# Seeding the first output of FFN layer 1 in PSUM from weight pair 3 on

## The chip, the cores and the metric

The kernel runs on one core of a Trainium2 chip. Its time is the device time of one execution in microseconds (us). Three runs of the kernel before took 1123.45, 1124.03 and 1124.14 us; the median, 1124.03 us, is the number that a change is held against. The engines are called as in the profile: PE (TensorE, matrix products; PEld is its weight load), DVE (VectorE), ACT (ScalarE), POOL (GpSimd), SP (SyncE, which issues the transfers).

## What is computed

One transformer block on 2048 tokens of width 576, in float32: a layer norm, then, side by side, a local attention (32 heads of 18, each token looks at 8 earlier tokens in steps of 2) and a feed-forward net with Mish, both added to the input.

```python
x = A_x
xn = _layernorm(x, axis=-1)
return x + _A_ref(xn, A_wqkv, A_wo) + _B_ref(xn, B_w1, B_b1, B_w2)

def _B_ref(x, w1, b1, w2):          # D = 576, F = 4608
    h = jnp.einsum("bsd,df->bsf", x, w1) + b1
    sp = jnp.log1p(jnp.exp(-jnp.abs(h))) + jnp.where(h > 0, h, jnp.zeros_like(h))
    act = h * jnp.tanh(sp)
    return jnp.einsum("bsf,fd->bsd", act, w2)
```

## The kernel before

**Halves, pairs, parts.** The tokens are worked through in two halves of 1024 (`hf` 0 and 1). In each half come first the products for q, k and v, then FFN layers 1 and 2 in 18 steps, one for each pair of weight blocks (`q` from 0 to 17, 256 of the 4608 columns each), and at the very end the output product of both halves. Every float32 factor is split into a high and a low part, so that one logical product of two row blocks is six matmuls (high·high, high·low, low·high, for two blocks): `prod`. The 64 rows that are left of 576 are two matmuls more: `rest`.

**Seven products instead of eight.** Within a pair, layer 1 makes four outputs (two blocks of 512 tokens, `b`, by two weight blocks, `j`), by Strassen's scheme in Winograd's form. `m1_part` issues its six parts. In part 0, a *shared product* goes into the PSUM bank `h1`, ACT copies it to SBUF (`take`, the tile `c11`), and a *second product* with its rest goes into another bank, `h2`. The first output is the sum of the two: `mish` is handed the bank and the copy, DVE adds the bank into the copy (L702), ACT applies Mish with the bias to the copy (L703), ACT casts its high part (L708) and POOL subtracts for the low part (L709). Part 1 puts the first of another pair of products, made with the weight sum `t1`, into the bank `h3`. Parts 2 to 5 go on adding into `h1` and `h3`; on the way two more copies of `h1` are taken (`c21`, `c22`) and added the same way. The last output of a pair needs no add: there `mish` is called without a copy (`fresh`), and Mish reads the bank itself. In pairs 1 to 8 of the second half (`seven`), the outputs stay unsplit in fixed SBUF tiles (`raw_act`), because layer 2 has a Strassen scheme of its own there (`u_high` on ACT and `u_low` on DVE or POOL make its factors, `p_item` its products).

**What sets the order.** Each engine works through its own queue in the order of the program. The program is a list, `plan`, of items for PE: the parts of layer 1 mixed with chunks of layer 2 (`m2_pair`, `m2_cols`, `p_item`). For q from 1 on, most pairs have parts 0 and 1 side by side and then chunks between the others. Everything else is hung on these items with `before(i, fn)`: casts of the next pair's weights, transfers, and the steps of the attention, which POOL, DVE and ACT work on beside the FFN. The steps of the attention are spread by a sum over the items' lengths (`PART` for the parts of layer 1), in `cuts`. An attention step's exponential goes into the list `soon` and is issued at the head of the next item. What `mish` does after its matmuls goes into `pend` and is issued at the next item, ahead of that item's own matmuls:

```python
    for i, (fns, bg, _) in enumerate(plan):
        first, soon[:] = soon[:], []
        held, pend[:] = pend[:], []
        for fn in first + bg + (fns + held if i == at["m", 0, 1, 0] else held + fns):
            fn()
```

So at part 0 of a pair, ACT's queue holds: an exponential if one is due, the casts that hang on this item, Mish and cast of the last output of the pair before, and then the copy of the shared product.

**PSUM.** `bank` draws from four banks ("h"): `h1` for the whole pair, `h2` and `h3` for a part of it; the fourth is the `h1` of the pair before or after. The layer 2 products have four banks of their own ("out"), which DVE empties with adds (L759, L853, L871).

Of the kernel before, what the change touches and what calls it, by code (L numbers as in the profile page):

```python
# [39 lines left out]
def block_kernel(ctx: ExitStack, tc: tile.TileContext, x, wq, wo, w1, b1, w2, mask, out):  # L40
    nc = tc.nc
# [605 lines left out]
    cur = {}  # L647
    late = []

    def bank(hf, q, n):  # L650
        cur[n] = ps.tile([P, TB], F32, tag="h", bufs=4, name=f"h{n}_{hf}_{q}")
        return cur[n]

    def prod(ph, wt, off, X, hi, lo, first, last):
        seq = [(off + k, wl, xs + k) for k in range(2) for wl, xs in ((0, hi), (0, lo), (1, hi))]
        for i, (wk, wl, xs) in enumerate(seq):
            nc.tensor.matmul(ph, wt[:, wl, wk * P:(wk + 1) * P], X[:, xs, :],  # L657
                             start=first and i == 0, stop=last and i == len(seq) - 1,
                             skip_group_check=True)

    def rest(ph, wt, off, X, xs):
        for wl in range(2):
            nc.tensor.matmul(ph, wt[:, wl, off * P:(off + 1) * P], X[:, xs, :], start=False, stop=wl == 1,  # L663
                             skip_group_check=True)

    seven = lambda hf, q: hf == 1 and q <= 2 * OC
    rawact, rslot, held_, owner, where = {}, {}, {}, {}, {}

    def raw_act(q, b, j):
        if not rslot:  # L670
            for n in range(4):
                rslot["raw", n] = sb.tile([P, 5 * P], F32, tag="raw", bufs=4, name=f"ra{n}")
            for n in range(5):
                rslot["mn", n] = sb.tile([P, D], F32, tag="mn", bufs=5, name=f"rm{n}")
            for n in range(2):
                rslot["tt", n] = sb.tile([P, 4 * P], F32, tag="tt", bufs=2, name=f"rt{n}")
        tag, n = {(0, 0): (("raw", 0), ("raw", 1), ("raw", 2)), (1, 0): (("mn", 2), ("mn", 3), ("mn", 0), ("r3", 0)),
                  (0, 1): (("raw", 3), ("mn", 4), ("mn", 1)), (1, 1): (("tt", 0), ("tt", 1))}[b, j][q % {(1, 0): 4, (1, 1): 2}.get((b, j), 3)]
        if (tag, n) not in rslot:
            rslot[tag, n] = sb.tile([P, 2 * 432], F32, tag="r3", bufs=1, name="ra_r")  # L680
        rawact[q, b, j] = rslot[tag, n][:, 0:TB]
        owner[tag, n] = q, b, j
        where[q, b, j] = tag, n
        return rawact[q, b, j]

    def take(hf, q, name):
        if seven(hf, q):
            t = cur[name] = raw_act(q, *dict(c11=(0, 0), c21=(1, 0), c22=(1, 1))[name])
        else:
            t = cur[name] = sb.tile([P, TB], F32, tag="mn", bufs=5, name=f"{name}_{hf}_{q}")  # L690
        nc.scalar.copy(t, cur[1])  # L691

    def mish(hf, q, b, j, ph, t=None):
        f = 2 * (Q1[q] if hf else q) + j
        n = f"{hf}_{b}_{f}"
        fresh = t is None
        if fresh:
            t = raw_act(q, b, j) if seven(hf, q) else sb.tile([P, TB], F32, tag="mn", bufs=5, name=f"mn_{n}")

        def run():  # L700
            if not fresh:
                nc.vector.tensor_tensor(out=t, in0=ph, in1=t, op=ALU.add)  # L702
            nc.scalar.activation(t, ph if fresh else t, AF.Mish, bias=b1c[:, f:f + 1])  # L703
            if seven(hf, q):
                held_[q, f"A{b + 1}{j + 1}"] = f"A{b + 1}{j + 1}"
                return
            a = acts[hf, q, b, j] = sb.tile([P, 2, TB], F32R, tag=f"a{b}", bufs=(3, 2)[b], name=f"act_{n}")
            nc.scalar.copy(a[:, 0, :], t)  # L708
            nc.gpsimd.tensor_tensor(out=a[:, 1, :], in0=t, in1=a[:, 0, :].bitcast(F32), op=ALU.subtract)  # L709
        if q or b != j:  # L710
            pend.append(run)
        else:
            late.append(run)

    def m1_part(hf, q, part):
        X0, X1 = XTs[hf, 0], XTs[hf, 1]
        if part == 5 and late:
            for fn in late[::-1]:
                fn()
            late.clear()  # L720
        wa, wc, t0, t1 = (done.get((k, hf, q)) for k in ("wa", "wc", "t0", "t1"))
        if part == 0:
            prod(bank(hf, q, 1), wa, 0, X0, 0, 5, True, True)
            take(hf, q, "c11")
            prod(bank(hf, q, 2), wa, 2, X0, 2, 7, True, False)
            rest(cur[2], wa, 4, X0, 4)
            mish(hf, q, 0, 0, cur[2], cur["c11"])
        elif part == 1:
            prod(bank(hf, q, 3), t1, 0, X1, 0, 5, True, True)
        elif part == 2:  # L730
            prod(cur[1], t0, 2, Ss[hf, 1], 0, 2, False, True)
            take(hf, q, "c21")
        elif part == 3:
            prod(cur[1], t0, 0, Ss[hf, 0], 0, 2, False, False)
            rest(cur[1], wc, 2, X1, 4)
            take(hf, q, "c22")
        elif part == 4:
            prod(cur[3], t1, 2, X1, 2, 7, False, False)
            rest(cur[3], wa, 4, X1, 4)
            mish(hf, q, 1, 0, cur[3], cur["c21"])  # L740
        else:
            prod(cur[1], wc, 0, Ss[hf, 2], 0, 2, False, False)
            rest(cur[1], wc, 2, X1, 9)
            mish(hf, q, 0, 1, cur[1])
        if part == 3:
            mish(hf, q, 1, 1, cur[3], cur["c22"])
# [388 lines left out]
    plan = []  # L1135
    at = {}
    US = {"q": 2.75, "z": 2.5, "p": 3.15, "t": 0.6, "o": 2.6}
    PART = (3.2, 1.4, 1.4, 1.8, 1.8, 1.8)

    def add(tag, *fns, alias=None):  # L1140
        at[tag] = at[alias] = len(plan)
        plan.append((list(fns), [], PART[tag[3]] if tag[0] == "m" else US[tag[0]]))

    def before(i, fn):
        plan[max(i, 0)][1].append(fn)
# [1 line left out]
    def qi(hf, g, b, jj, alias=None):  # L1147
        add(("q", hf, g, b, jj), lambda: qkv_item(hf, g, b, jj), alias=alias)

    def zi(jj, part):  # L1150
        add(("z", jj, part), lambda: z_part(1, jj, part))

    def mi(hf, q, part, alias=None):
        add(("m", hf, q, part), lambda: m1_part(hf, q, part), alias=alias)
# [337 lines left out]
    for n in range(2 * steps):  # L1492
# [4 lines left out]
        hf = n // steps  # L1497
# [86 lines left out]
```

## Time and profile before

| | before |
|---|---|
| median of three runs | 1124.03 us (1123.45 to 1124.14) |
| span of the profiled execution, first to last instruction | 1121.6 us |
| median less span | 2.4 us |
| DVE, ACT, POOL busy | 74%, 44%, 70% of the span |
| adds of a copy and a bank (L702) | 108 in all: 3 for each of 36 pairs |
| weight pairs with q of 3 or more | 15 in each half, 30 in all |

The page gives no time of its own for the profiled execution; its span is set against the median, and the 2.4 us between them are taken as what lies around the span. In the lists below a row of the timeline gives start, length, engine, line, operation, output and inputs, shape and count; in brackets stands how long the engine had been idle before, and what it waited for. A row of the waits gives engine, line, what was waited for, the total in us, how many times, and the longest.

### The profile page before, as it was taken

What the parts mean: (1) busy time and instruction counts of PE and PEld (TensorE: products, weight loads), DVE (VectorE), ACT (ScalarE), POOL (GpSimd) and SP (SyncE); (2) the same over time, 40 slices, a digit from 0 to 9 for tenths busy, and PEclk for the clock granted to TensorE, in tenths of its full rate; (3) what the DMA queues carried; (4) which work ended last, traced back from release to release, by engine and by line L of the source; (5) the groups of instructions that cost most, each with busy time, mean ns of one, the idle gap of its engine ahead of it and who ended that gap; (6) DMA issues with size and microseconds to landing.
All of it is one profiled execution on the core that took longest, in us unless ns stands there. A gap on an engine that the chain in (4) does not pass through costs nothing.

```text
span 1121.6 us, 18415 instructions
## 1 busy us (share of the span) xinstructions
PE 1109.5 (99%) x6630; PEld 1023.0 (91%) x6630; DVE 829.0 (74%) x1351; ACT 492.1 (44%) x892; POOL 787.7 (70%) x639
## 2 busy tenths in 40 slices
PE   8999999999999999999999999999999999999998
PEld 7999899999999999899999889999999999999998
DVE  6368788888888888877655456687866677776876
ACT  5544645544554545455233355343433343443332
POOL 2488767767689687676788476665789878668632
PEclk9999999999999999999999999999999999999999
DMA  6899885868767849666596797655655477676463
GB/s 200 283 312 318 290 283 205 289 228 284 261 240 258 282 163 345 222 240 214 191 342 238 231 373 249 241 200 174 227 198 189 168 263 269 215 253 248 157 222 104
DMA packets 147487, 271.08 MB, mean 242 GB/s; under 512 B 30114, under 2 KB 86724, under 8 KB 147396
## 3 DMA queue, kind: packets, MB, share of 16 engines
q1 hardware_dynamic: 147396, 269.91, 69.2%
q8 instruction: 52, 0.85, 0.3%
q14 instruction: 39, 0.32, 0.1%
HBM read 160.39 MB, written 109.48 MB: 241 GB/s over the span
## 4 chain that ended last, share of the span: by engine, by line
PE 89%; DVE 4%; POOL 3%; DMA 2%; issue 1%; ACT 1%; DVEq 0%; POOLq 0%; SPq 0%
PE h L657 28%; PE po L755 19%; PE pq L349 11%; PE po L868 10%; PE po L847 7%; PE h L663 5%; PE o L1056 4%; PE z L447 2%; DMA acc<-in_x 1%; POOL accP L856 1%; DVE u L801 1%; POOL pr L534 0%; DVE accP L871 0%; POOL act L709 0%; DMA z_B<-kept_wq 0%
## 5 line engine op out<-in xcount | busy, mean ns | idle before, releaser
L755 PEld LDWEIGHTS po<-w,act 128*128 128x128 f32 x1728 | 236.4, 188 | 7.5 <-DVE acc L759 1.7
L755 PE MATMUL po<-w,act 128*128 128x288 f32 x1728 | 240.8, 295 | 1.4 <-DVE acc L759 1.2
L534 POOL TENSOR_TENSOR pr<-q,kv 128x576 f32<-128x576 f32 x128 | 195.7, 1553 | 18.7 <-DMA q<-q_d 16.9
L572 POOL TENSOR_TENSOR pv<-L,kv 128x576 f32<-128x576 f32 x128 | 174.3, 1461 | 38.7 <-DVE L L565 20.9
L709 POOL TENSOR_TENSOR act<-c,act 128x512 fp32r<-128x512 f32 x81 | 107.1, 1322 | 128.4 <-ACT act L708 125.5
L759 DVE TENSOR_TENSOR acc<-po,acc 128x288 f32<-128x288 f32 x288 | 120.4, 450 | 31.6 <-PE po L755 30.2
L349 PE MATMUL pq<-wq,xt 128*128 128x432 f32 x672 | 136.2, 361 | 1.8 <-ACT xt L83 1.8
L868 PEld LDWEIGHTS po<-w,act 128*128 128x128 f32 x960 | 131.1, 188 | 3.7 <-DVE accP L871 0.4
L868 PE MATMUL po<-w,act 128*128 128x288 f32 x960 | 133.8, 295 | 0.2
L349 PEld LDWEIGHTS pq<-wq,xt 128*128 128x128 f32 x672 | 125.0, 188 | 8.7 <-ACT xt L83 2.7
L703 ACT ACTIVATE c<-c,b1c 128x512 f32<-128x512 f32 x81 | 58.7, 724 | 132.9 <-DVE c L702 132.6
L657 PE MATMUL h<-xt,t 128*128 128x512 f32 x432 | 110.6, 391 | 0.9 <-DVE c L702 0.8
L657 PE MATMUL h<-S,t 128*128 128x512 f32 x432 | 110.4, 391 | 0.0
L691 ACT COPY c<-h 128x512 f32<-128x512 f32 x81 | 47.4, 586 | 136.5 <-PE h L663 78.3
L578 DVE TENSOR_REDUCE og<-pv 128x144 f32<-128x1152 f32 x64 | 85.9, 1343 | 25.4 <-POOL pv L572 25.4
L657 PE MATMUL h<-xt,wa 128*128 128x512 f32 x432 | 104.0, 390 | 0.0
L657 PEld LDWEIGHTS h<-xt,wa 128*128 128x128 f32 x432 | 80.9, 188 | 16.9
L871 DVE TENSOR_TENSOR accP<-po,accP 128x288 f32<-128x288 f32 x160 | 69.6, 454 | 36.1 <-PE po L868 34.5
L847 PEld LDWEIGHTS po<-pw,u 128*128 128x128 f32 x672 | 92.4, 188 | 2.9 <-DVE u L801 0.5
L847 PE MATMUL po<-pw,u 128*128 128x288 f32 x672 | 94.2, 296 | 0.3 <-DVE u L801 0.3
L539 DVE TENSOR_REDUCE L<-pr 128x64 f32<-128x1152 f32 x64 | 85.8, 1341 | 11.2 <-POOL pr L534 11.1
L657 PEld LDWEIGHTS h<-xt,t 128*128 128x128 f32 x432 | 79.0, 188 | 16.1 <-DVE c L702 1.1
(231 smaller groups left out, 1840.5 us busy)
## 6 DMA issues: line engine op xcount, KB each, us to landing
kv<-kv_d SPq DMA_DIRECT2D x64, 396.0 KB, 5.2
kept_t<-t SPq DMA_DIRECT2D x36, 512.0 KB, 5.3
t<-kept_t SPq DMA_DIRECT2D x36, 512.0 KB, 5.4
rw<-in_w SPq DMA_DIRECT2D x36, 320.0 KB, 4.6
kept_wa<-wa SPq DMA_DIRECT2D x18, 640.0 KB, 3.5
kept_w<-w SPq DMA_DIRECT2D x20, 576.0 KB, 4.8
wa<-kept_wa SPq DMA_DIRECT2D x18, 640.0 KB, 6.1
w<-kept_w SPq DMA_DIRECT2D x20, 576.0 KB, 4.5
```

The source lines that it names most:

```text
L349: nc.tensor.matmul(pq[:, 0:432], XT[:, xi, tok], wt[wi][:, hl, 0:432], start=i == 0, stop=i == len(seq) - 1)
L534: nc.gpsimd.tensor_tensor(out=pr[:, x:x + hh], in0=q[:, j0 + x:j0 + x + hh, None, :].to_broadcast([P, hh, W, CU]), in1=win(kt, 0, CU, j0 + ...
L539: nc.vector.tensor_reduce(L[:, k, j0:j0 + hj].rearrange("p j w h -> p (j w h)"), pr.rearrange("p j w (h d) -> p (j w h) d", h=2), axis=AX, ...
L572: nc.gpsimd.tensor_tensor(out=pr[:, x:x + hj].rearrange("p j d w -> p j w d"), in0=L[:, k, x:x + hj, :, h:h + 1].to_broadcast([P, hj, W, DH]),
L578: nc.vector.tensor_reduce(og[:, :, c0:c0 + DH], pr, axis=AX, op=ALU.add)
L657: nc.tensor.matmul(ph, wt[:, wl, wk * P:(wk + 1) * P], X[:, xs, :], start=first and i == 0, stop=last and i == len(seq) - 1, skip_group_ch ...
L709: nc.gpsimd.tensor_tensor(out=a[:, 1, :], in0=t, in1=a[:, 0, :].bitcast(F32), op=ALU.subtract)
L755: nc.tensor.matmul(po, acts[hf, q, b, j][:, al, tok], done["w2", hf, 2 * q + j][:, wl, c * HC:(c + 1) * HC], start=i == 0, stop=i == 5)
L759: nc.vector.tensor_tensor(out=t, in0=po, in1=t, op=ALU.add)
L847: nc.tensor.matmul(po, units[e, k, qq][:, al, tok], w[:, qq, wl, :], start=i == 0, stop=i == 5)
L868: nc.tensor.matmul(po, acts[hf, q, b, j][:, al, tok], done["w2", hf, 2 * q + j][:, wl, c * HC:(c + 1) * HC], start=i == 0, stop=i == 5)
L871: nc.vector.tensor_tensor(out=t, in0=po, in1=t, op=ALU.add)
```

## The change

From pair 3 on (`seeded`), in both halves, part 0 ends after the shared product: ACT copies it from `h1` into the PSUM bank `h2`, not into SBUF. The second product and its rest move behind the product of part 1 and add into `h2` without a first matmul that starts the sum afresh. Mish is then called without a copy and reads `h2`. DVE's add of `c11` is gone in these 30 pairs. In `add`, the lengths of parts 0 and 1 change places for them, so that the sum that spreads the attention steps follows the moved matmuls.

```diff
     seven = lambda hf, q: hf == 1 and q <= 2 * OC
+    seeded = lambda q: q >= 3
...
         if part == 0:
             prod(bank(hf, q, 1), wa, 0, X0, 0, 5, True, True)
+            if seeded(q):
+                nc.scalar.copy(bank(hf, q, 2), cur[1])
+                return
             take(hf, q, "c11")
             prod(bank(hf, q, 2), wa, 2, X0, 2, 7, True, False)
             rest(cur[2], wa, 4, X0, 4)
             mish(hf, q, 0, 0, cur[2], cur["c11"])
         elif part == 1:
             prod(bank(hf, q, 3), t1, 0, X1, 0, 5, True, True)
+            if seeded(q):
+                prod(cur[2], wa, 2, X0, 2, 7, False, False)
+                rest(cur[2], wa, 4, X0, 4)
+                mish(hf, q, 0, 0, cur[2])
...
-        plan.append((list(fns), [], PART[tag[3]] if tag[0] == "m" else US[tag[0]]))
+        part = tag[3] ^ 1 if tag[0] == "m" and tag[3] < 2 and seeded(tag[2]) else tag[-1]
+        plan.append((list(fns), [], PART[part] if tag[0] == "m" else US[tag[0]]))
```

What this does to the queues is shown at three places. The names are the program's with a running number behind them: `h1_0_4` is the bank `h1` of half 0, pair 4. First PE at the start of pair 4 of half 0, before:

```order
L657 MATMUL h1_0_4_2225<-xt_0_0_231,wa_0_4_1960 128x512 x6
L657 MATMUL h2_0_4_2234<-xt_0_0_231,wa_0_4_1960 128x512 x6
L663 MATMUL h2_0_4_2234<-xt_0_0_231,wa_0_4_1960 128x512 x2
L657 MATMUL h3_0_4_2253<-xt_0_1_515,t1_0_4_2131 128x512 x6
L755 MATMUL po_0_3_1_0_0_2268<-w2_0_6_1927,act_0_1_6_2163 128x288 x3
```

and PE at the same place now:

```order
L657 MATMUL h1_0_4_2224<-xt_0_0_231,wa_0_4_1951 128x512 x6
L657 MATMUL h3_0_4_2238<-xt_0_1_515,t1_0_4_2130 128x512 x6
L657 MATMUL h2_0_4_2231<-xt_0_0_231,wa_0_4_1951 128x512 x6
L663 MATMUL h2_0_4_2231<-xt_0_0_231,wa_0_4_1951 128x512 x2
L763 MATMUL po_0_3_1_0_0_2266<-w2_0_6_1927,act_0_1_6_2162 128x288 x3
```

The same 20 matmuls stand before the first layer 2 matmul; the six into `h3` have moved ahead of the eight into `h2`. The same place on ACT, before (the first rows belong to an attention step that falls here: a table load, the exponential, and the table load back to Mish):

```order
L559 ACTIVATE L_0_1_1605<-L_0_1_1605 128x256
L256 CAST w2_0_8_2213<-rw2_8_2070 128x576
L703 ACT_TABLE_LOAD
L703 ACTIVATE mn_0_0_7_2211<-h1_0_3_1939,b1c_126 128x512
L708 CAST act_0_0_7_2222<-mn_0_0_7_2211 128x512
L691 COPY c11_0_4_2232<-h1_0_4_2225 128x512
L256 CAST wa_0_5_2246<-rw1_10_2135 128x640
L703 ACTIVATE c11_0_4_2232<-c11_0_4_2232,b1c_126 128x512
```

and ACT now:

```order
L559 ACTIVATE L_0_1_1605<-L_0_1_1605 128x256
L256 CAST w2_0_8_2212<-rw2_8_2069 128x576
L704 ACT_TABLE_LOAD
L704 ACTIVATE mn_0_0_7_2210<-h1_0_3_1939,b1c_126 128x512
L709 CAST act_0_0_7_2221<-mn_0_0_7_2210 128x512
L726 COPY h2_0_4_2231<-h1_0_4_2224 128x512
L256 CAST wa_0_5_2236<-rw1_10_2134 128x640
L256 CAST w2_0_9_2254<-rw2_9_2132 128x576
L704 ACTIVATE mn_0_0_8_2253<-h2_0_4_2231,b1c_126 128x512
```

The copy keeps its place behind the exponential and the last output of pair 3; only what it writes is another, and Mish on the first output comes one cast later. The third place is PE at pair 9 of half 1, where a layer 2 item, the products of `u_3_6_0` and `u_3_6_1`, lies between parts 0 and 1. Before:

```order
L657 MATMUL h1_1_9_9183<-xt_1_0_6031,wa_1_10_8828 128x512 x6
L657 MATMUL h2_1_9_9192<-xt_1_0_6031,wa_1_10_8828 128x512 x6
L663 MATMUL h2_1_9_9192<-xt_1_0_6031,wa_1_10_8828 128x512 x2
L847 MATMUL po_3_6_0_0_9224<-pw_3_6_9078,u_3_6_0_9090 128x288 x3
L847 MATMUL po_3_6_0_0_9224<-pw_3_6_9078,u_3_6_1_9092 128x288 x3
```

and now:

```order
L657 MATMUL h1_1_9_9162<-xt_1_0_6016,wa_1_10_8808 128x512 x6
L855 MATMUL po_3_6_0_0_9189<-pw_3_6_9057,u_3_6_0_9069 128x288 x3
L855 MATMUL po_3_6_0_0_9189<-pw_3_6_9057,u_3_6_1_9071 128x288 x3
L855 MATMUL po_3_6_0_1_9197<-pw_3_6_9057,u_3_6_0_9069 128x288 x3
L855 MATMUL po_3_6_0_1_9197<-pw_3_6_9057,u_3_6_1_9071 128x288 x3
```

The layer 2 item now comes right behind the six matmuls of the shared product, eight matmuls earlier than before.

On DVE, 30 rows are gone. The exponentials keep their places on ACT. A few attention steps move by an item or two: on POOL in pairs 8, 15 and 16 of half 0, on DVE a reduction (L578) in pair 15 of half 0, which stood ahead of four adds of layer 2 (L759) and now stands behind them. SP issues a few of the attention transfers some places later.

## The prediction

> **What bounds the kernel now.** I read the busy line of the page first, then the waits of PE, then PE's and ACT's timelines around the shared product.
>
> ```profile
> PE 1109.5 (99%) x6630; PEld 1023.0 (91%) x6630; DVE 829.0 (74%) x1351; ACT 492.1 (44%) x892; POOL 787.7 (70%) x639
> ```
>
> PE is busy in 1109.5 of 1121.6 us and its matmuls stay the same 6630. So the time moves only where PE waits: a new wait adds its whole length, a wait that goes takes its length away, and work that goes from DVE is worth nothing by itself. Two of the waits of before lie where the change reaches (waits: engine, line, what was waited for, total, count, longest):
>
> ```profile
> PE po L755 <- DVE acc L759: 1.2, 1, 1.2
> ...
> PE po L847 <- DVE u L801: 0.3, 1, 0.3
> ```
>
> An ordinary pair, pair 5 of half 0, on PE's and ACT's timelines:
>
> ```profile
> 212.74 2.88 PE L657 MATMUL h<-xt,wa 128*128 128x512 f32 x12
> 215.46 0.62 PE L663 MATMUL h<-xt,wa 128*128 128x512 f32 x2
> ```
> ```profile
> 214.30 0.59 ACT L691 COPY c<-h 128x512 f32<-128x512 f32 x1
> ```
>
> Twelve matmuls issue in 215.46 - 212.74 = 2.72 us, 0.227 each. The shared product is the first six (1.36 us). The copy ends at 214.89, which is 2.15 us after the pair's first matmul. Today PE doesn't need it. With the change the second product adds on top of the copy, so its first matmul waits for it; ahead of it stand the shared product and the six of part 1, 2 x 1.36 = 2.72 us. **The rule for each of the 30 pairs:** the copy must end by the pair's start + 2.72 us, and what is missing PE waits. Pair 5 keeps 0.57 us. The latest of the pairs without a table load ahead of the copy is pair 10:
>
> ```profile
> 333.36 2.88 PE L657 MATMUL h<-xt,wa 128*128 128x512 f32 x12
> ```
> ```profile
> 335.26 0.58 ACT L691 COPY c<-h 128x512 f32<-128x512 f32 x1
> ```
>
> Its copy ends 335.84 - 333.36 = 2.48 us after the start: 0.24 to spare.
>
> **Removed: 30 adds on DVE.**
>
> ```profile
> L702 DVE TENSOR_TENSOR c<-h,c 128x512 f32<-128x512 f32 x81 | 55.4, 686 | 33.1 <-ACT c L691 17.9 <-PE h L663 14.2
> ```
>
> 30 x 0.686 = 20.6 us less on DVE. DVE isn't the bound, and it comes back into step with PE at the next add of a layer 2 bank; so I cost this at nothing by itself, and count only where PE waits for DVE (below).
>
> **Added: a copy from PSUM to PSUM.** No row shows one. The nearest is the same copy to SBUF, 0.586 us on average, and I take that. The ends that I keep are 0.42 (the 128x256 activation in the list below) and 1.2, twice the row, as if PSUM at both ends cost double. At 0.42 each of the four late copies below would come 0.17 earlier, 0.6 us together. At 1.2 each of the four would come 0.6 later (2.4 us), and some 26 others would miss their place by 0.1 (0.61 more against some 0.5 us to spare; 2.4 us): 4.8 us.
>
> **Moved: the second product behind part 1.** Three kinds of place. (i) In most pairs nothing waits, as in pair 5. (ii) In four pairs ACT comes late. The clearest is pair 4 of half 0; PE, then ACT, then two rows of DVE:
>
> ```profile
> 188.66 2.88 PE L657 MATMUL h<-xt,wa 128*128 128x512 f32 x12
> ```
> ```profile
> 190.86 0.42 ACT L559 ACTIVATE L<-L 128x256 f32<-128x256 f32 x1 [1.99 <-DVE L L555]
> 191.19 0.66 ACT L256 CAST w<-rw 128x576 fp32r<-128x576 f32 x1
> 191.86 1.28 ACT L703 ACT_TABLE_LOAD   x1
> 193.16 0.69 ACT L703 ACTIVATE mn<-h,b1c 128x512 f32<-128x512 f32 x1
> 193.88 0.62 ACT L708 CAST act<-mn 128x512 fp32r<-128x512 f32 x1
> 194.41 0.58 ACT L691 COPY c<-h 128x512 f32<-128x512 f32 x1
> ```
> ```profile
> 172.42 0.46 DVE L759 TENSOR_TENSOR acc<-po,acc 128x288 f32<-128x288 f32 x1 [0.34 <-PE po L755]
> ...
> 190.40 0.43 DVE L555 TENSOR_TENSOR L<-L,m 128x256 f32<-128x256 f32 x1
> ```
>
> An exponential (L559) stands ahead of the copy, waits 1.99 us for DVE, and brings a table load behind it. The copy ends at 194.99; wanted is 188.66 + 2.72 = 191.38. **Wait: 3.61 us.** Would the exponential come earlier, with DVE's add of pair 3 gone? DVE waited for PE at 172.42, behind that add, so what the add leaves is lost again there; the add of pair 4 stands behind L555. I say no. What is queued behind ACT's copy (casts, Mish of the first output) is late by nothing, since the copy keeps its place. The three others, PE first, then ACT:
>
> ```profile
> 309.21 2.88 PE L657 MATMUL h<-xt,wa 128*128 128x512 f32 x12
> ...
> 453.91 2.88 PE L657 MATMUL h<-xt,wa 128*128 128x512 f32 x12
> ...
> 872.01 2.89 PE L657 MATMUL h<-xt,wa 128*128 128x512 f32 x12
> ```
> ```profile
> 311.45 0.58 ACT L691 COPY c<-h 128x512 f32<-128x512 f32 x1
> ...
> 456.60 0.58 ACT L691 COPY c<-h 128x512 f32<-128x512 f32 x1
> ...
> 876.29 0.57 ACT L691 COPY c<-h 128x512 f32<-128x512 f32 x1
> ```
>
> Pair 9 of half 0: 312.03 against 311.93, 0.10. Pair 15 of half 0: 457.18 against 456.63, 0.55. Pair 11 of half 1: 876.86 against 874.73, 2.13. There too DVE fell back into step with PE just before:
>
> ```profile
> 870.35 0.46 DVE L871 TENSOR_TENSOR accP<-po,accP 128x288 f32<-128x288 f32 x1 [0.28 <-PE po L868]
> ```
>
> (iii) In pair 9 of half 1 a layer 2 item lies between parts 0 and 1 and now starts eight matmuls sooner, while DVE still makes its factor:
>
> ```profile
> 820.21 2.89 PE L657 MATMUL h<-xt,wa 128*128 128x512 f32 x12
> ```
> ```profile
> 820.92 1.41 DVE L801 TENSOR_TENSOR u<-ra,u 128x512 fp32r<-128x512 f32 x1
> ```
>
> The item starts at 820.21 + 1.36 = 821.57; its third matmul, two steps of 0.13 later, needs the low part that DVE ends at 822.33: 0.49 us. The new waits: 3.61 + 0.10 + 0.55 + 2.13 + 0.49 = **6.88 us**.
>
> **Waits that go.** First pair 15 to 16 of half 0, PE and then DVE:
>
> ```profile
> 461.62 1.53 PE L657 MATMUL h<-S,t 128*128 128x512 f32 x6
> 464.40 3.46 PE L755 MATMUL po<-w,act 128*128 128x288 f32 x24 [1.25 <-DVE acc L759]
> ```
> ```profile
> 458.56 1.35 DVE L578 TENSOR_REDUCE og<-pv 128x144 f32<-128x1152 f32 x1 [2.40 <-POOL pv L572]
> ```
>
> PE could have gone on at 461.62 + 1.36 = 462.98 and did so at 464.40: 1.42 us. DVE's add was late because the reduction ahead of it waited 2.40 us for POOL. Now the reduction stands behind these adds, and the add of the copy is gone too. What is late next is the reduction's result, which the end of the attention needs far later. Second, in half 1, where DVE's add waited for PE and `u` stood behind it:
>
> ```profile
> 748.30 0.82 PE L847 MATMUL po<-pw,u 128*128 128x288 f32 x5
> 749.41 1.88 PE L847 MATMUL po<-pw,u 128*128 128x288 f32 x12 [0.29 <-DVE u L801]
> ```
> ```profile
> 747.21 0.69 DVE L702 TENSOR_TENSOR ra<-h,ra 128x512 f32<-128x512 f32 x1 [2.21 <-PE h L663]
> ```
>
> Five matmuls of 0.13 end the issue at 748.96, so 0.45 us goes. Together **1.87 us**; the sum of waits is 6.88 - 1.87 = +5.0 us.
>
> **PE's clock behind the longest wait.** Rows of the windows (us, busy of PE, PEld, DVE, ACT, POOL, granted clock, transfers):
>
> ```profile
> 1.34:4.92 3.58, 3.58 (x17) 3.58 (x18) 1.13 (x5) 0.66 (x1) 0.00 (x0) 1.00 0.82 241
> 4.92:1121.08 1116.16, 1105.91 (x6615) 1019.43 (x6613) 827.40 (x1347) 490.84 (x891) 786.97 (x633) 1.00 0.70 242
> 1121.08:1121.60 0.52, 0.00 (x0) 0.00 (x0) 0.00 (x0) 0.00 (x0) 0.00 (x0) 0.50 0.00 0
> 462.33:465.75 3.42, 2.17 (x14) 1.71 (x13) 3.42 (x7) 2.19 (x5) 3.25 (x5) 1.00 0.98 324
> ...
> 1117.66:1121.08 3.42, 0.70 (x6) 0.46 (x4) 0.59 (x2) 0.00 (x0) 0.00 (x0) 1.00 0.35 123
> ```
> ```profile
> 1117.93 0.43 PE L1056 MATMUL o<-wo_r,ob 128*128 128x288 f32 x2
> ```
>
> The clock is 1.00 until 1121.08 and then 0.50, 2.72 us after the last matmul ended (1118.36). So PE idle for 2.7 us can halve the clock; 3.42 us with PE busy in 2.17 did not. The new wait of 3.61 us is longer than the one, the 2.13 us of pair 11 lie between. At the start PE ran 17 small matmuls at 3.58/17 = 0.21 us for 3.58 us; if a return to full speed again takes as long, and up to 3.61 - 2.72 = 0.9 us of it still lies in the wait, the drop costs half of 2.7 to 3.6, 1.3 to 1.8. I take **1.6 us**, once, behind pair 4. [...]
>
> **The sum:** +5.0 + 1.6 = +6.6 us on the profiled execution: 1121.6 + 6.6 = 1128.2, and with the 2.4 us that the median has above the span 1130.6 us.
>
> **The rivals.**
> 1. The clock stays. [...] Then 1130.6 - 1.6 = 1129.0 us.
> 2. The copy into PSUM is dear: at 1.2 us the 4.8 from above come on top, 1135.4 us.
> 3. Not slower: DVE, 20.6 us lighter, runs ahead and hands the exponentials over sooner. The price is ACT's 1.99 us idle before L559 and what is like it in pair 11. It decides from the point where L555 ends at 188.9 and not 190.83; then pair 4 waits 3.61 - 1.9 = 1.7 us, the clock stays, and if pair 11 is covered likewise (2.13 - 1.9 = 0.2), the waits are 1.7 + 0.10 + 0.55 + 0.2 + 0.49 = 3.0 against 1.87: +1.2, 1125.2 us. Against it stand the waits of DVE for PE at 172.42 and 870.35.
> 4. All the copies are in time, since the waits shift the queues against each other; only the gains stay: 1124.03 - 1.87 = 1122.2, or with more waits for DVE gone below 1121.8.
>
> **How the numbers follow.** Forecast (clock falls once, or in pair 11 too, 1132) 0.50; rival 1 0.30; rival 2 0.03; rival 3 0.11; rival 4 0.06, of which I put 0.04 below 1121.8. A change of 0.2%, 2.25 us, is about what a measurement can tell from none: slower 0.83 (forecast, rivals 1 and 2), same 0.13 (rival 3 and 0.02 of rival 4), faster 0.04. The range of 8 in 10 holds the forecast and rival 1. At the low end stands rival 1 with copies of 0.42 and a gain of 1 us uncounted, 1127.2, and a part of rival 3: 1126.3. At the high end stand a second drop and copies somewhat dearer than 0.586: 1132.8.
>
> **What the profile after would show.** Right: among PE's waits a new one of PE `h` for ACT `h` with its longest near 3.6 us and a next one near 2.1; one of about 0.5 for `u`; none for `acc` near 466; 78 adds of a copy on DVE instead of 108; a granted clock below 1.00 for about 3 us near 195. Wrong: PSUM copies far from 0.59 us, or no PE wait at pairs 4 and 11, which would mean that the exponentials moved; or waits of PE in ordinary pairs such as 5, which would mean that the 2.72 us of cover don't hold.

## The result, and the profile after

| | before | after |
|---|---|---|
| median, five runs each | 1124.14 us (1123.45 to 1124.54) | 1130.94 us (1129.45 to 1133.48) |
| ratio | | 1.0066, 95% interval 1.0055 to 1.0077 |
| span of the profiled execution | 1121.6 us | 1127.7 us |

The kernel is 6.8 us slower. The page's line of the busy times, of after:

```profile
PE 1110.1 (98%) x6630; PEld 1023.0 (91%) x6630; DVE 818.9 (73%) x1321; ACT 490.4 (43%) x892; POOL 789.4 (70%) x639
```

DVE has lost 30 instructions and 10.1 us of busy time. That is half of the 20.6 us that the 30 adds made up; the other half came back in other rows, as in the adds of layer 2 into `acc` (122.7 us instead of 120.4) and L257 on `wq` (14.4 instead of 11.9). PE's 6630 matmuls are busy for 1110.1 us, 1109.5 before. The profiled execution took 1129.45 us, 1.8 us more than its span; so of the 2.4 us that were taken as lying around the span of before, some 0.6 are the distance of that execution from its median (the fastest of the three took 1123.45). The forecast doesn't change by this, since it is a difference on top of the median. The difference is in PE's waits (engine, line, what was waited for, total, count, longest):

```profile
PE h L657 <- ACT h L726: 5.6, 3, 3.4
PE o L1064 <- DVE y L1068: 1.8, 3, 0.7
...
PE h L657 <- DVE rt L703: 1.2, 1, 1.2
...
PE po L855 <- DVE u L809: 0.4, 1, 0.4
```

and the row for `y` of before:

```profile
PE o L1056 <- DVE y L1060: 1.3, 2, 0.7
```

The two waits of before that the prediction quotes (`acc` 1.2, `u` 0.3 near 749) are not there; in their place stand three waits for ACT's copy into `h`, one for `u` in another pair, and two that nobody had foreseen (`rt` and the third `y`). Pair 4 of half 0 on PE and then ACT, of after:

```profile
188.18 1.52 PE L657 MATMUL h<-xt,wa 128*128 128x512 f32 x6
189.54 1.52 PE L657 MATMUL h<-xt,t 128*128 128x512 f32 x6
194.47 1.66 PE L657 MATMUL h<-xt,wa 128*128 128x512 f32 x6 [3.40 <-ACT h L726]
```
```profile
190.30 0.42 ACT L559 ACTIVATE L<-L 128x256 f32<-128x256 f32 x1 [1.98 <-DVE L L555]
190.62 0.66 ACT L256 CAST w<-rw 128x576 fp32r<-128x576 f32 x1
191.29 1.28 ACT L704 ACT_TABLE_LOAD   x1
192.59 0.69 ACT L704 ACTIVATE mn<-h,b1c 128x512 f32<-128x512 f32 x1
193.31 0.62 ACT L709 CAST act<-mn 128x512 fp32r<-128x512 f32 x1
193.83 0.58 ACT L726 COPY h<-h 128x512 f32<-128x512 f32 x1
```

The shared product and the six of part 1 issue until 189.54 + 1.36 = 190.90; the second product starts at 194.47. The chain on ACT is the one of before, with the same wait for DVE at its head (1.98 us, 1.99 before). The other long wait is in pair 11 of half 1, PE and then ACT:

```profile
875.37 1.53 PE L657 MATMUL h<-xt,wa 128*128 128x512 f32 x6
876.75 1.52 PE L657 MATMUL h<-xt,t 128*128 128x512 f32 x6
880.00 1.66 PE L657 MATMUL h<-xt,wa 128*128 128x512 f32 x6 [1.73 <-ACT h L726]
```
```profile
876.39 0.42 ACT L559 ACTIVATE L<-L 128x256 f32<-128x256 f32 x1 [2.45 <-DVE L L555]
...
879.37 0.58 ACT L726 COPY h<-h 128x512 f32<-128x512 f32 x1
```

Taken from the start of one matmul to the start of the next, less the usual step of that shape, the new waits of PE are 3.56 (pair 4), 0.15 and 0.59 (pairs 9 and 15 of half 0), 1.89 (pair 11 of half 1), 0.57 (`u`): 6.8 us. Gone are 1.41 and 0.45. New and not foreseen are 1.2 for `rt` and 0.7 for `y`, against 0.6 us less in the first 16 us and 0.5 us in two short waits of before that are gone. The sum, +5.7 us, stands beside +6.1 of the spans. In this execution the granted clock stayed at 1.00, as two rows of the windows show (us, busy of PE, PEld, DVE, ACT, POOL, granted clock, transfers):

```profile
189.56:192.98 3.42, 1.50 (x7) 0.92 (x5) 1.64 (x3) 2.65 (x4) 2.02 (x3) 1.00 0.29 115
192.98:196.39 3.41, 1.93 (x8) 1.61 (x9) 1.29 (x2) 2.63 (x5) 2.39 (x2) 1.00 0.24 87
```

It was the fastest of five, and the only one with a mean clock of 1.000. The others, at 0.997 or 0.998, took 1130.44 to 1133.48 us.

### The profile page after: what moved, and what is told of

The parts are those of the page before. It is cut to its first block, busy times and chain, and to the rows that moved or that the text cites. A ratio compares the mean times of both kernels' runs of the same rounds, so it can differ in the third digit from the quotient of the medians.

```text
span 1127.7 us, 18324 instructions
## 1 busy us (share of the span) xinstructions
PE 1110.1 (98%) x6630; PEld 1023.0 (91%) x6630; DVE 818.9 (73%) x1321; ACT 490.4 (43%) x892; POOL 789.4 (70%) x639
## 4 chain that ended last, share of the span: by engine, by line
PE 91%; DVE 4%; ACT 2%; issue 1%; DMA 1%; POOL 0%; SPq 0%; DVEq 0%; ACTq 0%; POOLq 0%
PE h L657 28%; PE po L763 19%; PE pq L349 11%; PE po L876 10%; PE po L855 7%; PE h L663 5%; PE o L1064 4%; PE z L447 4%; DVE L L539 1%; DVE accP L879 1%; PE ta L77 0%; DMA acc<-in_x 0%; DVE og L578 0%; DMA kept_t<-t 0%; ACT L704 0%
## 5 line engine op out<-in xcount | busy, mean ns | idle before, releaser
L710 POOL TENSOR_TENSOR act<-c,act 128x512 fp32r<-128x512 f32 x57 | 75.2, 1319 | 126.7 <-ACT act L709 124.5
L767 DVE TENSOR_TENSOR acc<-po,acc 128x288 f32<-128x288 f32 x288 | 122.7, 451 | 47.4 <-PE po L763 46.3
L657 PE MATMUL h<-xt,wa 128*128 128x512 f32 x432 | 109.5, 391 | 5.6 <-ACT h L726 5.6
L578 DVE TENSOR_REDUCE og<-pv 128x144 f32<-128x1152 f32 x64 | 85.9, 1342 | 23.4 <-POOL pv L572 23.4
L539 DVE TENSOR_REDUCE L<-pr 128x64 f32<-128x1152 f32 x64 | 85.8, 1341 | 13.8 <-POOL pr L534 13.7
L692 ACT COPY c<-h 128x512 f32<-128x512 f32 x57 | 33.4, 586 | 140.1 <-PE h L663 79.3
L657 PEld LDWEIGHTS h<-S,t 128*128 128x128 f32 x432 | 77.9, 188 | 12.8
```

The source lines that it names most:

```text
L539: nc.vector.tensor_reduce(L[:, k, j0:j0 + hj].rearrange("p j w h -> p (j w h)"), pr.rearrange("p j w (h d) -> p (j w h) d", h=2), axis=AX, ...
L578: nc.vector.tensor_reduce(og[:, :, c0:c0 + DH], pr, axis=AX, op=ALU.add)
L767: nc.vector.tensor_tensor(out=t, in0=po, in1=t, op=ALU.add)
```

## The experiments

All are edits of the changed kernel or of the kernel before. Each is set against runs of before on the same chip, whose median was 1123.69 us for the first four, 1124.28 for the next four and 1123.93 for the last two.

**The changed kernel once more.** No edit.

> The changed kernel once more. Theory (late copies plus a clock that falls in some executions): the same waits of PE in the profile (3.5 us in pair 4 of half 0, 1.9 in pair 11 of half 1, 0.5 to 0.6 in pair 15 of half 0 and pair 9 of half 1), times spread over 2 us or more, and executions with a mean granted clock of 1.000 are at least 1.5 us shorter than those with 0.998 or less. Rival (the spread comes from transfers or the attention, not the clock): no such order between clock and time, and the waits of PE differ from profile to profile by more than 0.5 us.

1132.94 us (1131.69 to 1135.32), 1.0082 of before (1.0069 to 1.0095); all five executions had a mean clock of 0.995 to 0.998. PE's waits for the copies were the same 3.57, 0.59 and 1.88 us. The windows of this run:

```profile
191.80:195.22 3.42, 0.53 (x2) 0.48 (x3) 0.70 (x1) 3.38 (x6) 1.08 (x2) 1.00 0.24 89
195.22:198.63 3.41, 3.41 (x11) 2.77 (x10) 1.83 (x2) 1.19 (x3) 1.62 (x2) 0.50 0.52 182
198.63:202.04 3.41, 3.41 (x25) 3.32 (x25) 1.83 (x5) 1.28 (x3) 2.47 (x3) 1.00 0.28 97
...
352.23:355.64 3.41, 1.53 (x10) 1.07 (x9) 3.41 (x5) 0.58 (x1) 1.60 (x2) 1.00 1.02 415
355.64:359.06 3.42, 3.42 (x16) 3.42 (x15) 2.29 (x6) 2.09 (x4) 0.67 (x1) 0.50 1.04 409
```

The clock is halved for 3.41 us right behind pair 4's wait: 11 matmuls in that stretch, 25 in the next. A second fall follows a wait of 2.0 us at 353, for an add of layer 2 on DVE, which the first profile did not have. So the waits for copies agree between the two profiles, and the clock and the wait of 2.0 us for DVE differ between them. The expected order of clock and time could not be seen here, since no execution kept the full clock. In the first set the one execution that kept it was the shortest, by 1.0 to 4.0 us where at least 1.5 was expected; and those at 0.998 alone spread from 1130.44 to 1133.26, so the clock is not the whole of the spread.

**Without the five late pairs.**

```diff
+    seed = lambda hf, q: seeded(q) and (hf, q) not in ((0, 4), (0, 9), (0, 15), (1, 9), (1, 11))
...
-            if seeded(q):
+            if seed(hf, q):
```

> The change without five pairs (4, 9, 15 of half 0; 9, 11 of half 1), which keep the order and the add of before; 25 pairs stay seeded. Theory of late copies: 6.8 us of waits go and the clock stays, 1130.9 - 6.8 - 1.6 = 1122.5 us, 1.5 us below before, since the two waits that the change takes away stay away. Rival (each seeded pair pays for its copy into PSUM, its hand-over or the moved attention steps): 25 of 30 shares of 6.8 us stay, about 1129.8 us.

1122.14 us (twelve runs), 0.9983 of before (0.9974 to 0.9992). PE waits for no copy in its profile, with 25 pairs seeded. The whole loss goes with five pairs; the rival is out. The clock did not stay everywhere: two of the twelve executions, the 1124.25 and 1124.31 us, were at 0.998.

**Pair 4 of half 0 alone.**

```diff
+    seed = lambda hf, q: (hf, q) == (0, 4)
...
-            if seeded(q):
+            if seed(hf, q):
...
-        part = tag[3] ^ 1 if tag[0] == "m" and tag[3] < 2 and seeded(tag[2]) else tag[-1]
+        part = tag[3] ^ 1 if tag[0] == "m" and tag[3] < 2 and False else tag[-1]
```

> The kernel before with pair 4 of half 0 alone seeded, and the lengths that spread the attention as before. Theory: this one wait of 3.6 us, 1124.1 + 3.6 = 1127.7 us where the clock stays and 1129.4 where it falls, the median between them. Rival (a price for each seeded pair): a thirtieth of 6.8 us, 1124.4 us.

1129.47 us, 1.0051 (1.0039 to 1.0063): 5.8 us for one copy in one pair. All five executions were at a clock of 0.997 or 0.998. The wait is 3.63 us in the profile, and the clock cost another 1.7, an estimate for 3.41 us at half speed as in the run above, which agrees with the mean of 0.998 over this profile's 1129.7 us; the 0.5 that is left is within what the waits for DVE vary by (this profile has 1.4 and 1.3 us of those that the profile of before lacks). The median stands at the end where the clock falls, not between the two ends, and far from the rival's 1124.4.

**The wait filled with work.**

```diff
-            prod(bank(hf, q, 3), t1, 0, X1, 0, 5, True, True)
+            bank(hf, q, 3)
+            for k in range(30 if (hf, q) == (0, 4) else 0):
+                nc.tensor.transpose(cur[3][:, (k % 4) * P:(k % 4 + 1) * P], ident, ident)
+            prod(cur[3], t1, 0, X1, 0, 5, True, True)
```

> The change with 30 small matmuls (the identity, 128x128) into the bank of part 1 ahead of its product in pair 4 of half 0, whose sum starts afresh behind them: 30 x 0.109 = 3.3 us of PE work in place of PE's wait. Theory (the clock falls behind the wait of pair 4): the wait in pair 4 is 0.3 us, the time of the queues is as with the change, the clock is 1.00 in all executions, and the median is that of an execution with the clock in full, 1129.4 us, with a spread of 1 us as before. Rival (the clock falls behind another wait, or the spread has another cause): median 1130.9 us and a spread of 4 us as with the change.

1130.79 us (1129.22 to 1131.53), 1.0058 (1.0045 to 1.0071), 2.15 us below the changed kernel beside it (1132.94) although PE does 3.2 us more work (189.56 to 192.75). PE around the filled place:

```profile
188.19 1.53 PE L657 MATMUL h<-xt,wa 128*128 128x512 f32 x6
189.56 3.44 PE L735 MATMUL h<-ident 128*128 128x128 f32 x30
192.75 1.65 PE L657 MATMUL h<-xt,t 128*128 128x512 f32 x6
194.48 1.65 PE L657 MATMUL h<-xt,wa 128*128 128x512 f32 x6
```

The second product starts at 194.48, where it started without the filling (194.47): ACT sets the time, not PE. Three of five executions kept a clock of 1.000, against none of the five of the changed kernel beside them, so the fall behind pair 4 is at least mostly gone. The expectation held only in part: two executions were at 0.998, and the median is 1.4 us above the 1129.4 expected and close to the rival's 1130.9. Where the clock fell in the two was not seen. Pair 11's wait may do it (1.69 of 3.42 us busy in the profile, no fall there), but executions at 0.998 also stand among those of the run without the late pairs. And one of the three at 1.000 took 1131.29 us, where the other two took 1129.22 and 1129.34, so something besides the clock moves the time by 2 us.

**The exponential behind the copy.**

```diff
-        for fn in first + bg + (fns + held if i == at["m", 0, 1, 0] else held + fns):
+        steps_ = [fn for fn in bg if fn in att_fns]
+        if first and i in part0:
+            order = [fn for fn in bg if fn not in att_fns] + held + fns + first + steps_
+        else:
+            order = first + bg + (fns + held if i == at["m", 0, 1, 0] else held + fns)
+        for fn in order:
             fn()
```

(`att_fns` lists the attention's steps, `part0` the items that are part 0 of a seeded pair; two of them have an exponential due. A step of the attention that hangs on such an item goes behind the copy as well.)

> The change, but in the two pairs where an exponential is due at part 0 (pair 4 of half 0, pair 11 of half 1) ACT gets it behind the copy instead of ahead; all 30 pairs stay seeded. Theory (the price is what stands ahead of the copy on ACT): the waits of 3.6 and 1.9 us fall to 0.3 or less, the clock stays at 1.00, the waits of 0.15, 0.6 and 0.55 stay; the sum is 1.3 - 1.9, up to 1.2 more if POOL and DVE still meet near 670: -0.6 to +0.6 us against before, 1123.1 to 1124.3. Rival (seeding itself costs): at least +5 us stay, 1129 or more.

1124.16 us (eleven runs), 1.0001 (0.9992 to 1.0010). ACT at pair 4 of this run:

```profile
188.64 0.69 ACT L704 ACTIVATE mn<-h,b1c 128x512 f32<-128x512 f32 x1 [0.80 <-PE h L663]
189.36 0.62 ACT L709 CAST act<-mn 128x512 fp32r<-128x512 f32 x1
190.00 0.57 ACT L726 COPY h<-h 128x512 f32<-128x512 f32 x1
190.59 1.28 ACT L559 ACT_TABLE_LOAD   x1
191.88 0.42 ACT L559 ACTIVATE L<-L 128x256 f32<-128x256 f32 x1
```

The copy ends at 190.57, 2.13 us after the pair's first matmul (188.44), as in an ordinary pair, and PE doesn't wait in pair 4 or 11. All 30 pairs are seeded and the loss against before is gone: two exponentials ahead of two copies were the price. The clock was expected to stay at 1.00; two of the eleven executions, the two longest, were at 0.998.

**The order without the seed.**

```diff
-                nc.scalar.copy(bank(hf, q, 2), cur[1])
+                take(hf, q, "c11")
...
-                prod(cur[2], wa, 2, X0, 2, 7, False, False)
+                prod(bank(hf, q, 2), wa, 2, X0, 2, 7, True, False)
                 rest(cur[2], wa, 4, X0, 4)
-                mish(hf, q, 0, 0, cur[2])
+                mish(hf, q, 0, 0, cur[2], cur["c11"])
```

> The order of the change without the seed: the second product behind that of part 1 in the 30 pairs, but with the copy in SBUF and DVE's add of before. Theory: no matmul waits for a copy, the wait of 0.55 for u in pair 9 of half 1 stays, the wait for the reduction near 463 stays away (the moved spread of the attention takes it away): 1123.7 + 0.55 - 1.4 = 1122.9 us. Rival (the moved matmuls and attention steps are what costs): 1127 or more.

1124.11 us, 0.9999 (0.9991 to 1.0008). No wait for a copy, so the rival is out, but 1.2 us above what was expected: the profile has waits for DVE of 0.73 near 197, 1.30 near 669 and 0.43 near 758 that no sum held. The wait of 1.4 near 463 is gone.

**The seed without the order.**

```diff
             if seeded(q):
                 nc.scalar.copy(bank(hf, q, 2), cur[1])
+                prod(cur[2], wa, 2, X0, 2, 7, False, False)
+                rest(cur[2], wa, 4, X0, 4)
+                mish(hf, q, 0, 0, cur[2])
                 return
...
-            if seeded(q):
-                prod(cur[2], wa, 2, X0, 2, 7, False, False)
-                rest(cur[2], wa, 4, X0, 4)
-                mish(hf, q, 0, 0, cur[2])
...
-        part = tag[3] ^ 1 if tag[0] == "m" and tag[3] < 2 and seeded(tag[2]) else tag[-1]
+        part = tag[3] ^ 1 if tag[0] == "m" and tag[3] < 2 and False else tag[-1]
```

> The seed without the order: in the 30 pairs the second product stands right behind the shared one and adds on top of ACT's copy in PSUM; the lengths that spread the attention as before. The cover is 1.36 us instead of 2.72. Theory: every pair waits, an ordinary one for 2.15 + 0.05 - 1.36 = 0.84 us (26 x 0.84 = 21.8), the four late ones for 4.9, 3.3, 1.9 and 1.5 (11.6), the clock falls once (1.7): 1123.7 + 35 = 1159 us. Rival (a copy into PSUM is dearer, or a matmul that adds on top of it starts later by x): 30 times x more.

1166.23 us, 1.0369 (1.0354 to 1.0384). An ordinary pair (pair 3 of half 0) on PE, and PE's waits for the copies in all, of this run:

```profile
164.08 1.52 PE L657 MATMUL h<-xt,wa 128*128 128x512 f32 x6
166.26 1.65 PE L657 MATMUL h<-xt,wa 128*128 128x512 f32 x6 [0.66 <-ACT h L726]
```
```profile
PE h L657 <- ACT h L726: 29.6, 30, 5.5
```

164.08 + 1.36 = 165.44, and 166.26 is 0.82 later; 0.84 was expected. All 30 pairs wait, so the six matmuls of part 1 are what covers the copy. The 29.6 us count the idle time alone; with the 0.16 that each start lies later than the idle shows, they are 34.4 us against 33.4 expected. Most of the 7 us above 1159 is the clock: in the profiled execution it was at half not once for 3.41 us but for 13.7 us in all, which agrees with its mean of 0.994 over 1164.7 us. PE was idle for 1.4 of the first 6.83 of these anyway, so they cost an estimated 6 us instead of 1.7. The wait for `rt` (1.3) is there too. The clock fell at the ends of the first, third and fourth of these windows; the last is the stretch at half behind the third:

```profile
191.43:194.84 3.41, 0.00 (x0) 0.00 (x0) 1.53 (x3) 2.74 (x4) 1.92 (x3) 1.00 0.00 0
194.84:201.67 6.83, 5.44 (x13) 4.28 (x14) 1.23 (x2) 3.55 (x7) 1.48 (x2) 0.50 0.52 182
474.74:478.15 3.41, 1.62 (x8) 1.01 (x7) 1.22 (x2) 2.84 (x6) 3.05 (x3) 1.00 0.41 170
904.81:908.23 3.42, 0.92 (x5) 0.41 (x3) 1.55 (x4) 2.98 (x5) 1.09 (x1) 1.00 1.02 403
478.15:481.56 3.41, 3.41 (x10) 2.63 (x9) 3.22 (x3) 1.64 (x3) 3.33 (x6) 0.50 0.03 8
```

PE was busy for 0.00, 1.62 and 0.92 us in the three. Behind the first the clock stayed at half for 6.83 us, of which PE was busy for 5.44. A copy into PSUM took 572 ns, one into SBUF 586; by form, in this run:

```profile
L692 ACT COPY c<-h 128x512 f32<-128x512 f32 x57 | 33.4, 586 | 172.6 <-PE h L657 90.4 <-PE h L663 82.3
...
L726 ACT COPY h<-h 128x512 f32<-128x512 f32 x30 | 17.2, 572 | 6.0 <-PE h L657 5.7
```

**Exponentials behind the copy, and three pairs unseeded.** The edit of the run above with the exponentials, and

```diff
+    seed = lambda hf, q: seeded(q) and (hf, q) not in ((0, 9), (0, 15), (1, 9))
...
-            if seeded(q):
+            if seed(hf, q):
```

> As the run with the exponentials behind the copy, and pairs 9 and 15 of half 0 and 9 of half 1 unseeded: 27 pairs seeded, none late. Theory: only the gains stay, 1123.7 - 1.9 = 1121.8 us or up to 1 us less, as in the run without the five late pairs (1122.1). Rival (the deferred exponentials make POOL or DVE late further on): above 1123.7.

1121.75 us (twelve runs), 0.9978 (0.9970 to 0.9987): 2.5 us below before, with 27 pairs seeded. It is the fastest version that was run, though its interval overlaps those of the run without the late pairs and of the next one. One of the twelve executions was at 0.998.

**The spread of the attention alone.** Of the changed kernel only the exchanged lengths stay.

```diff
-            if seeded(q):
-                nc.scalar.copy(bank(hf, q, 2), cur[1])
-                return
...
-            if seeded(q):
-                prod(cur[2], wa, 2, X0, 2, 7, False, False)
-                rest(cur[2], wa, 4, X0, 4)
-                mish(hf, q, 0, 0, cur[2])
```

> The kernel before with nothing but the exchanged lengths of parts 0 and 1, which move a few attention steps; no seed, no moved matmul. Theory: the wait of 1.4 us near 463 goes, since the reduction stands behind the adds of layer 2, and the 0.45 us near 749 stay: 1124.0 - 1.4 = 1122.6 us. Rival (the wait goes only with DVE's add of the copy): as before, 1124.0 us.

1122.64 us, 0.9988 (0.9979 to 0.9997), as the first theory said: the 1.4 us near 463 belong to the moved reduction, and DVE's add of the copy has no part in them. The 0.42 near 748 stay.

This run seeds nothing and stands 1.3 us below its before. The run without the five late pairs has the same lengths and 25 seeded pairs, and stands at 0.9983; the run before this one, with 27, at 0.9978. All three intervals overlap. So the moved attention steps alone can account for most of what those two runs gain. That seeding by itself gains anything is not shown by the times; in the profiles, the wait of 0.42 near 748 is gone in both of the seeded runs.

**The kernel before once more.**

> The kernel before once more, for a second profile of it. Theory (the wait of 1.0 to 1.4 us near 670, for a DVE subtraction that starts just behind a POOL one, is no part of the change): it can stand in a profile of before too. Rival (it comes with the change): 0.2 us there, as in the first profile.

No such wait in this profile either (DVE's subtraction L555 takes 0.42 us and POOL's starts 0.37 us behind it), so the expectation was not met. Neither theory holds as put. Among the other runs the wait stands also in two whose attention steps lie as before (pair 4 alone, and the seed without the order) and in the run with the spread alone, at 1.2 us; the run without the late pairs and the one with the exponentials behind the copy, which have the seed, the order and the moved steps, don't have it.

## Why the prediction was right

It said 1130.6 us, and the median was 1130.94. The mechanism held: late copies in the places that were named make PE wait, and the clock fell in nine of ten executions, in the profile that shows it right behind the longest wait. That the number agrees to 0.3 us is in part luck: the second five executions gave 1132.94, just above the 1132.8 at which the stated range ends. Point by point:

1. **What bounds it.** PE's waits, one for one. This held: the new waits less the old ones give 5.7 of the 6.1 us by which the spans differ, and filling the longest with 3.2 us of PE work moved the second product by 0.01 us.
2. **The rule of 2.72 us of cover.** This held in both directions: no ordinary pair waits with it, and with 1.36 us of cover all 30 do, an ordinary one for 0.82 us where the rule gives 0.84.
3. **The copy into PSUM**, taken at 0.586 us, took 0.572 in the seed without the order, 0.014 us less.
4. **The late pairs**, forecast at 3.61, 0.10, 0.55, 2.13 and 0.49 us, took 3.56, 0.15, 0.59, 1.89 and 0.57. Pair 11 is the one that moved: the copy there ended 4.58 us after the pair's start instead of 4.85. The third rival wanted exponentials that come sooner by some 1.9 us; in pair 4 that was nothing, in pair 11 these 0.27.
5. **The waits that go**, 1.42 and 0.45, are both gone. The prediction gave the add of the copy a part in the first; the moved reduction alone does it.
6. **The clock.** Its mean was 0.995 to 0.998 in nine of the ten executions of the changed kernel, the second profile shows the fall right behind pair 4, and 3.41 us at half speed are an estimated 1.7 us, where 1.6 was taken. The first rival, that the clock stays, is the profiled execution itself: it took 1129.45 us where that rival says 1129.0, with PE busy for 1.50 and 1.93 us in its two rows of 3.42 and 3.41 us. What was too cautious is the 2.7 us of idle time that the prediction went by: in the 3.41 or 3.42 us ahead of the falls shown above, PE was busy for 0.53 and 1.53 us (the changed kernel once more) and for 0.00, 1.62 and 0.92 us (the seed without the order). No fall stands behind the rows with 1.50 and 1.93 us of the profiled execution, nor behind the one with 1.69 us where the wait is filled. So the busy time does not sort the cases near 1.5 (1.50 without a fall, 1.53 with one); the ends of matmuls are modelled, and what else decides about the clock was not shown.

Two side sums of the prediction are slightly off and touch neither forecast nor range: 26 pairs late by 0.1 are 2.6 us and not 2.4, and rival 1 with cheap copies and a gain of 1 us comes to 1127.4 and not 1127.2.

What the sum left out came to +0.8 us in the profiled execution: 1.9 of new waits less 1.1 that went. The largest is the wait for `rt` near 673. DVE and POOL there, of after:

```profile
672.15 1.67 DVE L555 TENSOR_TENSOR L<-L,m 128x256 f32<-128x256 f32 x1
673.74 0.68 DVE L703 TENSOR_TENSOR rt<-h,rt 128x512 f32<-128x512 f32 x1
```
```profile
672.12 1.41 POOL L841 TENSOR_TENSOR accP<-accP,accP 128x576 f32<-128x576 f32 x1 [0.77 <-DMA accP<-in_x]
```

and at the same place of before:

```profile
669.49 0.43 DVE L555 TENSOR_TENSOR L<-L,m 128x256 f32<-128x256 f32 x1
```
```profile
669.64 1.56 POOL L833 TENSOR_TENSOR accP<-accP,accP 128x576 f32<-128x576 f32 x1 [0.95 <-DMA accP<-in_x]
```

POOL's subtraction waits for a transfer. In before it starts 0.15 us behind DVE's, and DVE takes 0.43 us; in after it starts 0.03 us ahead, DVE takes 1.67, and PE waits 1.24 us for the add behind it. Five more profiles give both rows at this place. In three of them (before once more, the run without the late pairs, the run with the exponentials behind the copy) DVE's instruction starts first, by 0.37, 0.38 and 0.14 us, and takes 0.42 us. In two (27 pairs seeded, the spread alone) POOL's starts first, by 0.25 and 0.09 us, and DVE's takes 1.45 and 1.62; it ends 0.28 or 0.29 us behind POOL's, as in after. In the other five profiles PE waits for `rt` too, for 0.8 to 1.3 us. What decides which of the two starts first stays open; the moved attention steps don't, as two runs without them have the wait too.

In the second measurement the changed kernel stood 9.2 us above before, not 6.8. Its profile there has a second fall of the clock and a wait of 2.0 us for DVE that the first lacks; that these make the difference in the median too is an inference from one profile.

## What to carry to other kernels

Before a matmul is made to wait for another engine, list for each place what stands ahead of the releasing instruction on its queue, not how long that instruction takes: 26 of 30 places were free, and two cost nearly everything. A wait of PE can cost more than its length: behind one of 2.0 us near 353 (the changed kernel once more) the clock was at half for 3.42 us. So the longest new wait deserves to be worked out alone. And undo a change place by place before giving it up or crediting it: with two exponentials moved and three pairs left out, the kernel stood 2.5 us below before instead of 6.8 above, but a kernel with no seed at all, and only the attention steps moved, stood 1.3 us below.

## What the runs showed that was not expected

- PE's clock fell at the end of stretches of 3.41 us of which PE was idle for only about half: it was busy for 1.53 us in one (the changed kernel once more) and for 1.62 us in another (the seed without the order). The clock then stayed at half for 3.42 and 3.41 us, an estimated 1.7 us lost where PE was busy throughout. Behind the longest wait of the seed without the order it stayed at half for 6.83 us, of which PE was busy for 5.44. Behind the wait in pair 4 the clock was at half for 3.41 us in one profile of the changed kernel (3.57 us of waiting) and at 1.00 in the other (3.56); why they differ was not shown.
- A DVE subtraction of 128x256 near 670 took 0.42 or 0.43 us in the four profiles where it started 0.14 to 0.38 us ahead of a POOL instruction, and 1.45 to 1.67 us in the three where it started 0.03 to 0.25 us behind it. That is up to 1.2 us for one instruction, and PE paid it: 1.24 us of waiting in the profile after.
